# A decode-attention kernel rewritten as a hand-ordered pipeline over blocks of 4 heads, with the softmax shift taken from GpSimd to TensorE

## The chip, the cores and the metric

The kernel runs on one core of a Trainium2 chip. The metric is device time in microseconds (us), as the median of several executions. A run more than 1.5% above the fastest of its kernel counts as slow, and is left out of the times below. Runs were made on several chips of the same kind, and the kernel before was always run again beside the new one: its median was 8688 us at first.

Engines in the profiles: PE is TensorE, PEld its weight load, DVE is VectorE, ACT is ScalarE, POOL is GpSimd, SP issues the DMA transfers. POOLq is GpSimd's sequencer, which takes the instructions in. The granted clock is the share of TensorE's full clock that the throttle let through, as the profile reports it.

## The reference

Two independent attention blocks, A and B, each decode one token for a batch of 8 with 32 heads, over a cache of 4096 keys of 128 elements, all in bf16:

```python
q = (x @ wq)                                    # 8 x 1024 @ 1024 x 4096, then (8, 32, 1, 128)
scores = einsum("bhqd,bhkd->bhqk", q, k_cache) * (128 ** -0.5)
p = softmax(scores)                             # over 4096 keys
o = einsum("bhqk,bhkd->bhqd", p, v_cache)
out = o.reshape(8, 1, 4096) @ wo                # 8 x 1024; A and B are joined on the last axis
```

There are 2 x 8 x 32 = 512 (block, batch, head) units. Each reads its own K and V, 1 MiB each, exactly once. With the weights that is 1107 MB, and nothing can be reused.

## The kernel before

K of a unit lies in SBUF as 128 partitions x 32 keys x 128 elements. The scores are made by a DVE multiply with the broadcast query (L452), a DVE add that folds 128 elements to 64 (L469), four PE matmuls with the identity that sum groups of 16 (L477), and a DVE reduce of the last 16 (L484). Then comes the softmax, for each unit by itself, and PV in eight PE matmuls (L541) into one column tile (the output partitions that `tile_position` names):

```python
o1 = g.add("dve", lambda e: e.tensor_reduce(rmax[:, ur:ur + 1], src, AX.X, ALU.max), ...)           # L505
o2 = g.add("pool", lambda e: e.partition_all_reduce(gmax[:, ur:ur + 1], rmax[:, ur:ur + 1], 128,
                                                    bass.bass_isa.ReduceOp.max), ...)               # L507
o3 = g.add("pool", lambda e: e.tensor_scalar(negb[:, ur:ur + 1], gmax[:, ur:ur + 1],
                                             -scale, None, ALU.mult), ...)                          # L510
o4 = g.add("act", lambda e: e.activation(pT[:, u % PR, :], src, ACTF.Exp, bias=negb[:, ur:ur + 1],
                                         scale=scale, accum_out=rsum[:, ur:ur + 1]), ...)           # L513
...
for gq in range(g0, g1):
    last = e.matmul(pbank[32 * q4:32 * q4 + 4, 0:512], pT[:, u % PR, 4 * gq:4 * gq + 4],            # L541
                    V_sb[:, vslot, gq * 512:(gq + 1) * 512],
                    start=(gq == 0), stop=(gq == NG - 1), tile_position=(0, 32 * q4))
```

o2 and o3 run both on GpSimd, one after the other. The first is a reduction over the 128 partitions. The second multiplies 128 numbers by a constant. Once per head (8 units) GpSimd also adds up the softmax sums with a `partition_all_reduce` (L521).

The order of the instructions on each engine is found by a list scheduler in the kernel's source. It is given a duration for each operation: 0.45 us for the all-reduce, 0.22 us for negb. K has 8 slots in SBUF and V 6, the scores have 3, and each transfer brings two units.

Of the kernel before, what the change touches and what calls it, by code (L numbers as in the profile page):

```python
# [13 lines left out]
class _Op:  # L14
    __slots__ = ("eng", "emit", "deps", "dur", "name", "prio", "dma_key", "nbytes",
                 "token", "sig", "start", "end", "done", "idx", "nsched", "users", "slack", "lock")

    def __init__(self, eng, emit, deps, dur, name, prio, dma_key=None, nbytes=0):
        self.eng = eng
        self.emit = emit  # L20
        self.deps = [d for d in deps if d is not None]
        self.dur = dur
        self.name = name
        self.prio = prio
        self.dma_key = dma_key
        self.nbytes = nbytes
        self.token = None
        self.sig = False
        self.start = None
        self.end = None  # L30
        self.done = None
        self.idx = None
        self.nsched = 0
        self.users = []
        self.slack = 0.0
        self.lock = (eng == "pool")


class _Graph:
    def __init__(self):  # L40
        self.ops = []

    def add(self, eng, emit, deps=(), dur=0.1, name="", prio=0.0, dma_key=None, nbytes=0):
        op = _Op(eng, emit, list(deps), dur, name, prio, dma_key, nbytes)
        self.ops.append(op)
        return op


def _schedule(ops, cfg):
    SEM_LAT = cfg.get("sem_lat", 0.15)  # L50
    DMA_US_PER_MB = cfg.get("dma_us_per_mb", 2.72)
    DMA_LAT = cfg.get("dma_lat", 1.4)
    DMA_MARGIN = cfg.get("dma_margin", 5.0)
    W_EXTRA = cfg.get("w_extra", 25.0)
    for i, op in enumerate(ops):
        op.idx = i
        op.nsched = 0
        op.users = []
    for op in ops:
        for d in op.deps:  # L60
            d.users.append(op)
    eng_free = {e: 0.0 for e in ENGINES}
    dma_free = [0.0]
    lock_free = [0.0]
    avail = {e: [] for e in ENGINES}
    for op in ops:
        if not op.deps:
            avail[op.eng].append(op)
    order = {e: [] for e in ENGINES}
    n_left = len(ops)  # L70
    while n_left:
        best = None
        best_key = None
        for e in ENGINES:
            lst = avail[e]
            if not lst:
                continue
            ef = eng_free[e]
            for op in lst:
                r = 0.0  # L80
                for d in op.deps:
                    t = d.done + SEM_LAT
                    if t > r:
                        r = t
                r += op.slack
                st = r if r > ef else ef
                if op.lock and lock_free[0] > st:
                    st = lock_free[0]
                if e == "sp":
                    kt = dma_free[0] - DMA_MARGIN  # L90
                    key = (st if st > kt else kt, op.prio, op.idx, st)
                else:
                    key = (st, op.prio, op.idx, st)
                if best_key is None or key < best_key:
                    best_key = key
                    best = op
        op = best
        e = op.eng
        st = best_key[3]
        op.start = st  # L100
        op.end = st + op.dur
        eng_free[e] = op.end
        if op.lock:
            lock_free[0] = op.end
        if op.dma_key is not None:
            s0 = max(dma_free[0], op.end + (DMA_LAT if dma_free[0] < op.end else 0.2))
            s1 = s0 + op.nbytes / 1048576.0 * DMA_US_PER_MB
            dma_free[0] = s1
            op.done = s1 + 0.3
            if op.dma_key == "w" and op.slack > 0:  # L110
                op.done += W_EXTRA
        else:
            op.done = op.end
        avail[e].remove(op)
        order[e].append(op)
        n_left -= 1
        for u in op.users:
            u.nsched += 1
            if u.nsched == len(u.deps):
                avail[u.eng].append(u)  # L120
    if cfg.get("verbose"):
        print("SCHED makespan", max(op.done for op in ops), {e: round(sum(o.dur for o in order[e]), 1) for e in ENGINES})
    return order


def _build_kernel(nc, caches, out, cfg):
    NK = cfg.get("NK", 8)
    NV = cfg.get("NV", 6)
    PR = cfg.get("PR", 8)
    SR = cfg.get("SR", 3)  # L130
    AR = cfg.get("AR", 3)
    MW = cfg.get("MW", 64)
    TREE = cfg.get("tree", 1)
    EVS = cfg.get("evac_splits", 2)
    kinds_pat = cfg.get("kinds", "F")
    PAIR = cfg.get("pair", True)
    if PAIR:
        assert NK % 2 == 0 and NV % 2 == 0

    x0, k0, v0, wq0, wo0 = caches[0]  # L140
    B, Sq, D = x0.shape
    _, H, Sk, Dh = k0.shape
    assert Sq == 1 and Dh == 128 and Sk == 4096 and D % 128 == 0
    T = Sk // 128
    G = 4
    DC = D // 128
    HD = H * Dh
    N = B * H
    NC = len(caches)
    NT = NC * N  # L150
    assert NT <= 512 and N % 4 == 0 and (4 % B == 0 or B % 4 == 0)
    scale = float(Dh) ** -0.5
    WH = cfg.get("w_parts", 2)
    assert H % WH == 0
    HP = H // WH
    WSZ = max(DC * HP * Dh, HP * D)
    PW = min(512, D)
    NPH = D // PW
    assert D % PW == 0 and 2 * N <= 512

    kind = [kinds_pat[u % len(kinds_pat)] for u in range(NT)]
    if "P" in kinds_pat:
        for u in range(max(0, NT - cfg.get("tail_p", 2)), NT):
            kind[u] = "P"
        for u in range(min(NT, cfg.get("head_p", 1))):
            kind[u] = "P"
    else:
        for u in range(max(0, NT - cfg.get("tail_e", 4)), NT):
            kind[u] = "E"
        for u in range(min(NT, cfg.get("head_e", 2))):  # L170
            kind[u] = "E"
    p_units = [u for u in range(NT) if kind[u] == "P"]
    d_units = [u for u in range(NT) if kind[u] in "DEF"]
    e_units = [u for u in range(NT) if kind[u] in "EF"]
    e_index = {u: i for i, u in enumerate(e_units)}
    HAS_P = bool(p_units)
    assert not (HAS_P and e_units), "P and E units are mutually exclusive (PSUM budget)"
    p_index = {u: i for i, u in enumerate(p_units)}
    d_index = {u: i for i, u in enumerate(d_units)}

    es = ExitStack()
    with es:
        block = es.enter_context(nc.Block())
        sb = lambda name, shape, dt: es.enter_context(nc.sbuf_tensor(name, shape, dt))
        ps = lambda name, shape, dt: es.enter_context(nc.psum_tensor(name, shape, dt))
# [3 lines left out]
        selA = sb("selA", [128, 128], BF16)  # L189
        selB = sb("selB", [128, 128], BF16)  # L190
        E4 = sb("E4", [128, 4, 4], BF16)
        QB = sb("QB", [128, NC * WH, 4 * HP * B + MW], BF16)
        accS = sb("accS", [128, AR, 512], BF16)
        x_sb = sb("x_sb", [B, NC, D], BF16)
        xT_sb = sb("xT_sb", [128, NC * DC * B], BF16)
        W_sb = sb("W_sb", [128, WSZ], BF16)
        qT_sb = sb("qT_sb", [128, NC, N], BF16)
        K_sb = sb("K_sb", [128, NK, T * Dh], BF16)
        V_sb = sb("V_sb", [128, NV, T * Dh], BF16)
        KT_sb = sb("KT_sb", [128, 2, T * 128], BF16) if HAS_P else None  # L200
        NPB = cfg.get("prod_bufs", 2)
        prod = sb("prod", [128, NPB, T * Dh], BF16)
        qbc = sb("qbc", [128, 2, 4, 128], BF16)
        s_sb = sb("s_sb", [128, SR, T], FP32)
        RS = min(NT, cfg.get("stat_ring", 64))
        assert RS % B == 0 and RS >= 4 * B
        rmax = sb("rmax", [128, RS], FP32)
        gmax = sb("gmax", [128, RS], FP32)
        negb = sb("negb", [128, RS], FP32)
        rsum = sb("rsum", [128, RS], FP32)  # L210
        Lall = sb("Lall", [128, RS], FP32)
        pT = sb("pT", [128, PR, T], BF16)
        rl = sb("rl", [128, 4, B], FP32)
        oacc = sb("oacc", [B, NC, D], FP32)
        on_sb = sb("on_sb", [128, NC, H, B], BF16)
        orow = sb("orow", [B, NC, D], BF16)

        RB = cfg.get("red_banks", 3)
        if HAS_P:
            kt_all = ps("kt_all", [128, 4, 512], FP32)  # L220
            sc = [ps(f"sc{i}", [128, 512], FP32) for i in range(2)]
            ktb_all = kt_all.bitcast(BF16)
            red_ps = None
        else:
            kt_all = ktb_all = None
            red_ps = ps("red_ps", [128, RB, 512], FP32)
            sc = [None, ps("sc1", [128, 512], FP32)]
            if cfg.get("acc_banks", 2) == 2 and RB <= 3:
                sc.append(ps("sc2", [128, 512], FP32))
# [6 lines left out]
        for e in ENGINES[1:]:  # L236
            sems[e] = es.enter_context(nc.semaphore(f"c_{e}"))
# [548 lines left out]
```

## Time and profile before

| | before |
|---|---|
| time, median | 8688 us |
| per unit (divided by 512) | 17.0 us |
| DVE busy | 2145 us, 25% |
| PE busy | 2577 us, 30% |
| packets of the main DMA queue | 32.2% of 16 engines' time, 127 GB/s mean |

No engine is near its limit. These are lines of the page of before: the span, busy time by engine, the main DMA queue, the shares of the chain of waits, and the groups of PV, GpSimd's two groups and exp. A group's line ends with the idle time of its engine just before it, and with what ended most of that idle time.

```profile
span 8728.2 us, 23766 instructions
PE 2576.8 (30%) x7848; PEld 630.1 (7%) x7848; DVE 2145.2 (25%) x2211; ACT 583.7 (7%) x1665; POOL 623.9 (7%) x1104
...
q1 hardware_dynamic: 152448, 1107.40, 32.2%
...
issue 67%; PE 15%; DVE 8%; POOL 7%; ACT 3%; POOLq 1%; DMA 0%; SPq 0%; DVEq 0%; ACTq 0%
...
L541 PE MATMUL sc<-V_sb,pT 128*4 128x512 bf16 x4096 | 1541.1, 580 | 4944.0 <-ACT pT L513 4907.5
...
L507 POOL PARTITION_ALL_REDUCE gmax<-rmax x512 | 455.7, 890 | 3077.8 <-issue 1364.1
...
L513 ACT ACTIVATE pT<-s_sb,negb 128x32 bf16<-128x32 f32 x512 | 164.5, 321 | 6630.9 <-POOL negb L510 6630.9
L510 POOL TENSOR_SCALAR negb<-gmax 128x1 f32<-128x1 f32 x512 | 138.7, 271 | 4624.5 <-issue 4624.5
...
```

"issue" is time for which the profile shows no instruction and no wait. It is 67% of the chain. PE waits for exp and exp waits for negb. Before negb GpSimd is silent for 4624.5 us, 9.0 us per unit, and before the all-reduce for 3077.8 us, 6.0 us per unit.

This is the chain of waits of before over one unit, in order of time: start, length, what.

```profile
4007.48 0.27 POOL negb L510
4007.75 0.02 issue
4007.77 0.42 ACT pT L513 x2
4008.19 0.04 issue
4008.24 1.87 PE sc L541 x4
4010.10 1.83 PE red_ps L477 x4
4011.94 0.02 issue
4011.96 0.70 DVE s_sb L484
4012.66 0.96 issue
4013.63 0.40 POOL gmax L507
4014.02 0.07 POOLq L510 x2
4014.10 6.88 issue
4020.97 0.27 POOL negb L510
```

It looks like a ring: negb, exp, PV, the next unit's score matmuls (their operand was ready at 4000.42, but they stand behind PV on PE), the reduce, the all-reduce, silence, negb. Two lines of the timeline show that the maximum of the scores reduced at 4011.96 is taken only after the all-reduce has begun:

```profile
4013.63 0.40 POOL L507 PARTITION_ALL_REDUCE gmax<-rmax  x1 [5.89 <-DVE s_sb L484]
...
4013.70 0.18 DVE L505 TENSOR_REDUCE rmax<-s_sb 128x1 f32<-128x32 f32 x1
```

That all-reduce works on the maximum before, which had been ready since 4000.58, for 13.0 us. Over the whole trace, with maxima and all-reduces matched in order, 478 of the 512 all-reduces start more than 10 us after their maximum was ready (17.0 us in the median). So the maxima wait for GpSimd, and from 4007.75 to 4013.63 something else must have kept GpSimd, which shows nothing there. What it is, the chain cannot say.

### The profile page before, as it was taken

What the parts mean: (1) busy time and instruction counts of PE and PEld (TensorE: products, weight loads), DVE (VectorE), ACT (ScalarE), POOL (GpSimd) and SP (SyncE); (2) the same over time, 40 slices, a digit from 0 to 9 for tenths busy, and PEclk for the clock granted to TensorE, in tenths of its full rate; (3) what the DMA queues carried; (4) which work ended last, traced back from release to release, by engine and by line L of the source; (5) the groups of instructions that cost most, each with busy time, mean ns of one, the idle gap of its engine ahead of it and who ended that gap; (6) DMA issues with size and microseconds to landing.
All of it is one profiled execution on the core that took longest, in us unless ns stands there. A gap on an engine that the chain in (4) does not pass through costs nothing.

```text
span 8728.2 us, 23766 instructions
## 1 busy us (share of the span) xinstructions
PE 2576.8 (30%) x7848; PEld 630.1 (7%) x7848; DVE 2145.2 (25%) x2211; ACT 583.7 (7%) x1665; POOL 623.9 (7%) x1104
## 2 busy tenths in 40 slices
PE   2232233222232323223332232332323223233233
PEld 0000000000000000000000000000000000000000
DVE  2222222222222222222222222222222222222221
ACT  0000000000000000000000000000000000000000
POOL 0000000000000000000000000000000000000000
PEclk6556656565555655656555555555555555556556
DMA  5332323233332323323233333323333332323231
GB/s 231 135 144 107 134 115 135 115 126 124 135 135 116 135 116 128 122 115 135 116 140 129 118 132 122 129 116 122 128 134 135 127 123 116 135 116 135 116 135 58
DMA packets 152571, 1108.91 MB, mean 127 GB/s; under 512 B 9056, under 2 KB 9056, under 8 KB 21376
## 3 DMA queue, kind: packets, MB, share of 16 engines
q1 hardware_dynamic: 152448, 1107.40, 32.2%
q8 instruction: 62, 1.02, 0.0%
q14 instruction: 61, 0.50, 0.0%
HBM read 1107.33 MB, written 0.03 MB: 127 GB/s over the span
## 4 chain that ended last, share of the span: by engine, by line
issue 67%; PE 15%; DVE 8%; POOL 7%; ACT 3%; POOLq 1%; DMA 0%; SPq 0%; DVEq 0%; ACTq 0%
PE sc L541 7%; PE red_ps L477 7%; POOL gmax L507 5%; DVE s_sb L484 3%; DVE prod L469 3%; DVE prod L452 2%; ACT pT L513 2%; POOL negb L510 2%; PE misc L630 1%; ACT accS L548 1%; POOLq L510 0%; DVE rmax L505 0%; POOL Lall L521 0%; DVE oacc L640 0%; ACT qbc L668 0%
## 5 line engine op out<-in xcount | busy, mean ns | idle before, releaser
L541 PE MATMUL sc<-V_sb,pT 128*4 128x512 bf16 x4096 | 1541.1, 580 | 4944.0 <-ACT pT L513 4907.5
L484 DVE TENSOR_REDUCE s_sb<-red_ps 128x32 f32<-128x512 f32 x512 | 352.4, 688 | 4856.1 <-PE red_ps L477 4856.1
L452 DVE TENSOR_TENSOR prod<-K_sb,qbc 128x4096 bf16<-128x4096 bf16 x512 | 1166.2, 2281 | 28.7 <-ACT qbc L668 28.0
L477 PE MATMUL red_ps<-prod,ident 128*128 128x512 bf16 x2072 | 922.8, 600 | 446.3 <-DVE prod L469 429.5
L541 PEld LDWEIGHTS sc<-V_sb,pT 128*4 128x4 bf16 x4096 | 321.5, 105 | 6075.1 <-ACT pT L513 5205.9
L507 POOL PARTITION_ALL_REDUCE gmax<-rmax x512 | 455.7, 890 | 3077.8 <-issue 1364.1
L469 DVE TENSOR_TENSOR prod<-prod 128x2048 bf16<-128x2048 bf16 x506 | 614.1, 1217 | 1.4
L513 ACT ACTIVATE pT<-s_sb,negb 128x32 bf16<-128x32 f32 x512 | 164.5, 321 | 6630.9 <-POOL negb L510 6630.9
L510 POOL TENSOR_SCALAR negb<-gmax 128x1 f32<-128x1 f32 x512 | 138.7, 271 | 4624.5 <-issue 4624.5
L606 DVE RECIPROCAL rl<-Lall 128x8 f32<-128x8 f32 x64 | 13.0, 203 | 1538.0 <-POOL Lall L521 1538.0
L548 ACT ACTIVATE accS<-sc 4x512 bf16<-4x512 f32 x512 | 300.3, 586 | 1325.4 <-PE sc L541 1322.0
L477 PEld LDWEIGHTS red_ps<-prod,ident 128*128 128x128 bf16 x2072 | 223.2, 128 | 1074.1 <-issue 565.0
L556 PE MATMUL o_ps<-E,accS 128*128 128x4 bf16 x512 | 33.5, 170 | 635.3 <-ACT accS L548 635.3
L513 ACT ACTIVATION_READ_ACCUMULATOR pT<-s_sb,negb 128x1 f32 x512 | 95.3, 186 | 0.0
L505 DVE TENSOR_REDUCE rmax<-s_sb 128x1 f32<-128x32 f32 x512 | 91.6, 179 | 2.1
L668 ACT ACTIVATE qbc<-misc 128x512 bf16<-128x512 f32 x128 | 75.7, 592 | 181.3 <-PE misc L662 175.8
L662 PE MATMUL misc<-ident,qT_sb 128*128 128x128 bf16 x512 | 67.1, 273 | 58.0 <-ACT qbc L668 38.8
L556 PEld LDWEIGHTS o_ps<-E,accS 128*128 128x128 bf16 x512 | 24.1, 103 | 719.2 <-ACT accS L548 713.1
L630 PE MATMUL misc<-W_sb,on_sb 128*8 128x512 bf16 x128 | 55.5, 576 | 49.5 <-DVE on_sb L610 35.7
L521 POOL PARTITION_ALL_REDUCE Lall<-rsum x64 | 27.3, 426 | 387.7 <-issue 308.4
L662 PEld LDWEIGHTS misc<-ident,qT_sb 128*128 128x128 bf16 x512 | 39.1, 118 | 129.5 <-ACT qbc L668 55.5
L640 DVE TENSOR_TENSOR oacc<-oacc,misc 8x512 f32<-8x512 f32 x28 | 18.9, 675 | 48.9 <-PE misc L630 48.9
(25 smaller groups left out, 63.4 us busy)
## 6 DMA issues: line engine op xcount, KB each, us to landing
K_sb<-in_A_k_cache_dram SPq DMA_DIRECT2D x128, 2048.0 KB, 12.3
V_sb<-in_A_v_cache_dram SPq DMA_DIRECT2D x128, 2048.0 KB, 7.6
K_sb<-in_B_k_cache_dram SPq DMA_DIRECT2D x126, 2048.0 KB, 12.3
V_sb<-in_B_v_cache_dram SPq DMA_DIRECT2D x126, 2048.0 KB, 7.5
W_sb<-in_A_wq_dram SPq DMA_DIRECT2D x16, 512.0 KB, 13.9
W_sb<-in_B_wq_dram SPq DMA_DIRECT2D x16, 512.0 KB, 8.6
W_sb<-in_A_wo_dram SPq DMA_DIRECT2D x8, 1024.0 KB, 11.1
W_sb<-in_B_wo_dram SPq DMA_DIRECT2D x8, 1024.0 KB, 10.4
```

Of the source, the lines that this page charges most:

```text
L452: lambda e: e.tensor_tensor(pv_, K_sb[:, kslot, :].rearrange("p (t d) -> p t d", d=Dh), qbc[:, gi % 2, i, :].unsqueeze(1).to_broadcast([12 ...
L469: lambda e: e.tensor_tensor(pv_[:, :, 0:Dh // 2], pv_[:, :, 0:Dh // 2], pv_[:, :, Dh // 2:Dh], ALU.add),
L477: last = e.matmul(red_ps[:, rb, :].rearrange("p (t w) -> p t w", w=EW), ident[:], pj[:, :, jq, :], start=(jq == 0), stop=(jq == nj - 1))
L484: lambda e: e.tensor_reduce(s_sb[:, di % SR, :], red_ps[:, rb, :].rearrange("p (t w) -> p t w", w=EW), AX.X, ALU.add),
L505: o1 = g.add("dve", lambda e: e.tensor_reduce(rmax[:, ur:ur + 1], src, AX.X, ALU.max), [opScore[u], opArmax.get(u - RS)], 0.22, f"rmax{u}" ...
L507: o2 = g.add("pool", lambda e: e.partition_all_reduce(gmax[:, ur:ur + 1], rmax[:, ur:ur + 1], 128, bass.bass_isa.ReduceOp.max), [o1, opNeg ...
L510: o3 = g.add("pool", lambda e: e.tensor_scalar(negb[:, ur:ur + 1], gmax[:, ur:ur + 1], -scale, None, ALU.mult), [o2, opExp.get(u - RS)], 0 ...
L513: o4 = g.add("act", lambda e: e.activation(pT[:, u % PR, :], src, ACTF.Exp, bias=negb[:, ur:ur + 1], scale=scale, accum_out=rsum[:, ur:ur ...
L541: last = e.matmul(pbank[32 * q4:32 * q4 + 4, 0:512], pT[:, u % PR, 4 * gq:4 * gq + 4], V_sb[:, vslot, gq * 512:(gq + 1) * 512], start=(gq ...
L548: opAcc[u] = g.add("act", lambda e: e.activation(accS[32 * q4:32 * q4 + 4, ring, :], pbank[32 * q4:32 * q4 + 4, 0:512], ACTF.Copy), [opPV[ ...
L630: last = e.matmul(misc[0:B, 0:PW], on_sb[:, c, hh, :], W_sb[:, hl * D + ph * PW: hl * D + (ph + 1) * PW], start=(hh == h0), stop=(hh == h1 ...
L662: last = e.matmul(misc[:, i * 128:(i + 1) * 128], qT_sb[:, cc, jj:jj + 1].to_broadcast([128, 128]), ident[:], start=True, stop=True)
```

## The change

Its intent is to make one fixed order by hand in place of the scheduler's, with PV 6 units behind the multiply; to make the shift for 4 units at once, and on TensorE (a transpose of the 128x4 row maxima, a DVE max, and a tiny matmul that broadcasts and multiplies by -scale) in place of GpSimd; and to put the eight PV matmuls of a unit in four column tiles, to run side by side. The softmax sums also go to a PE matmul with ones. wq is loaded for 4 heads at a time (1 KB packets). The diff replaces nearly the whole builder, so only its core is shown:

```diff
-    NK = cfg.get("NK", 8)
-    NV = cfg.get("NV", 6)
-    PR = cfg.get("PR", 8)
-    SR = cfg.get("SR", 3)
+    LAG = 6
+    NK, NV, NP = 8, 8, 3
+    PR = 8
+    SG = 3
...  (softmax shift)
-            o2 = g.add("pool", lambda e: e.partition_all_reduce(gmax[:, ur:ur + 1], rmax[:, ur:ur + 1], 128, bass.bass_isa.ReduceOp.max),
-            o3 = g.add("pool", lambda e: e.tensor_scalar(negb[:, ur:ur + 1], gmax[:, ur:ur + 1], -scale, None, ALU.mult),
+        def make_tr(g):
+            opTr[g] = add("pe", lambda e: e.transpose(misc[0:HB, 0:128], rmax[:, g % 2, :], ident32[:]),
+                          [opRmax[g], c_ident32, last["misc"]])
+        def make_gm(g):
+            opGm[g] = add("dve", lambda e: e.tensor_reduce(gm[:, g % 2:g % 2 + 1], misc[0:HB, 0:128], AX.X, ALU.max),
+                          [opTr[g], _at(opNegb, g - 2)])
+        def make_exp(g):
+            opNegb[g] = add("pe", lambda e: e.matmul(misc[:, 128:128 + HB], gm[:, g % 2:g % 2 + 1].to_broadcast([HB, 128]),
+                                                     nid[:], start=True, stop=True), [opGm[g], c_nid])
+            opNegS[g] = last["misc"] = add("act", lambda e: e.activation(negb[:, g % 2, :], misc[:, 128:128 + HB], ACTF.Copy),
+                                           [opNegb[g], _at(opExp, HB * (g - 2) + HB - 1)])
...  (PV)
-                        last = e.matmul(pbank[32 * q4:32 * q4 + 4, 0:512], pT[:, u % PR, 4 * gq:4 * gq + 4], V_sb[:, vslot, gq * 512:(gq + 1) * 512],
-                                        start=(gq == 0), stop=(gq == NG - 1), tile_position=(0, 32 * q4))
+                for r in range(2):
+                    for q in range(4):
+                        gq = 2 * q + r
+                        i = e.matmul(bank[32 * q:32 * q + 4, :], pT[:, u % PR, 4 * gq:4 * gq + 4],
+                                     V_sb[:, u % NV, gq * 512:(gq + 1) * 512],
+                                     start=(r == 0), stop=(r == 1), tile_position=(0, 32 * q))
...  (order)
-        order = _schedule(g.ops, cfg)
+        for s in range(NT + LAG + 4):
+            if s < NT:
+                make_mul(s)
...  (K loads)
+            if 0 <= s - LAG < NT:
+                u = s - LAG
+                make_pv(u)
...  (V loads)
+            if 1 <= s <= NT:
+                make_red(s - 1)
+            if r4 == 1 and 1 <= g4 <= NG:
+                make_gm(g4 - 1)
+                make_exp(g4 - 1)
...
+            if s < NT:
+                make_eacc(s, make_fold(s))
+            if r4 == 0 and 1 <= g4 <= NG:
+                make_rmax(g4 - 1)
+                make_tr(g4 - 1)
...
```

## The prediction

> **What bounds the kernel now.** No engine does: the page's first part gives PE 30%, DVE 25%, ACT 7%, POOL 7%, and DMA packets 32% of 16 engines' time. 8688 us over 512 (batch, head) units is 17.0 us per unit. It is a latency ring through GpSimd. The chain of waits from 4000 to 4060 us repeats one loop per unit: exp 0.42 us, four PV matmuls 1.87, four score matmuls (L477) 1.83, score reduce (L484) 0.69, often the fold 1.14, PARTITION_ALL_REDUCE issued 0.4, then 6.9 or 11.1 us of "issue", then negb 0.27. The waits view sums the silence before negb to 4624.5 us, 9.0 per unit; "issue" is 67% of the chain. I read it as all-reduce time not recorded. PE runs in order and has the next unit's score matmuls behind this unit's PV, which waits for exp, so the latency is paid on every unit.
>
> **What the change does.** The 512 GpSimd all-reduces and 512 negb become, for each 4 units, a PE transpose, a DVE max, a tiny matmul and an ACT copy. PV of a unit runs 6 units behind its multiply, so this latency lies beside two or more steps of DVE work.
>
> **Work per unit afterwards (durations of the trace).**
> - DVE: multiply 2.28 + fold 1.22 + reduce 0.69 + about 0.14 (larger rmax and new gm, estimates from the 0.18 us rmax) = 4.33 us, some 4.5 with gaps: 2220 us busy, 2300 if it bounded.
> - PE: eight PV matmuls took 3.7 us cold; four column tiles side by side should need about 1 us (estimate; the Trainium skill, "TensorE: Matmul & The Clock Gate", Part 3, measures 2.38x for three; no run here shows it yet). With score matmuls at most 1.9 us and small work, 2.5 to 3.3 us.
> - ACT: exp 0.51, accS 0.59, qbc and negb 0.2: 1.3 us.
> - DMA: bytes are the same, 1107 MB. From 20 to 60 us the trace shows a saturated stretch: DMA share 1.01, 417 to 420 GB/s. So 2.10 MB per unit take 5.02 us.
>
> DMA becomes the bound. The skill's "HBM Reference", Access, gives about 425 GB/s for a core streaming alone; the trace agrees. 1107 MB at 418 is 2650 us. The wq loads fall to 1 KB packets; 2, 4 and 8 KB packets take 84, 159 and 309 ns (medians), so 1 KB should take about 46: wq and wo together add some 11 us. Start 5 us, tail 10 us. Sum 2676; for imperfect saturation I say 2700 us, 3.2 times faster.
>
> Range 2640 to 2880: the upper end is 385 GB/s sustained.
>
> **Signs.** DMA share at 0.97 or more and 405 to 420 GB/s in nearly all of the 40 slices; POOL under 10 us; the chain mostly DMA and PE/DVE links with K_sb or V_sb DMA as releasers, no POOL; DVE busy about 2220 us (82%), its largest wait the K_sb DMA before the multiply; PV matmuls of one unit spanning about 1 us; K landing times rising from 12 us to 25 or more.
>
> **What would make it wrong.** Sustained HBM rate below the 40-us stretch; the ring of 4 K and 4 V pairs on one in-order issue queue not keeping requests outstanding; column tiles not overlapping, with PE at the low clock (5.6 us per unit, then PE-bound near 2900); DVE stretched past 5 us by semaphore waits between dependent instructions; the transpose chain outlasting the pipeline's slack.

## The result, and the profile after

The kernel after takes 2664.0 us (median of 4 runs, 2663.85 to 2664.39), the kernel before beside it 8696.8 us. The ratio is 0.3063 (95% interval 0.3054 to 0.3072). The prediction was 2700 us, with a range of 2640 to 2880.

Lines of the page of after: span, busy time, the DMA engines' busy tenths and GB/s in 40 slices, the main queue, the chain's shares, and groups on DVE and PE.

```profile
span 2662.3 us, 22669 instructions
PE 1603.4 (60%) x9008; PEld 444.1 (17%) x9008; DVE 2103.0 (79%) x1829; ACT 575.2 (22%) x1811; POOL 4.1 (0%) x18
...
DMA  9999999999999999999999999999999999999998
GB/s 393 414 421 421 421 415 417 421 422 421 414 419 421 421 421 411 419 421 422 421 410 419 421 421 421 412 419 421 421 421 411 419 421 421 421 421 418 421 421 340
...
q1 hardware_dynamic: 164320, 1107.40, 100.6%
...
DMA 89%; PE 5%; DVE 4%; SPq 1%; issue 1%; ACT 0%; DVEq 0%
...
L237 DVE TENSOR_TENSOR prod<-K_sb,qbc 128x4096 bf16<-128x4096 bf16 x512 | 1170.0, 2285 | 110.7 <-DMA K_sb<-in_A_k_cache_dram 59.7
L297 PE MATMUL pv<-V_sb,pT 128*4 128x512 bf16 x4096 | 516.2, 581 | 846.4 <-DMA V_sb<-in_B_v_cache_dram 424.9
...
```

The DMA engines are full from the first slice to the last. 1107 MB at 421 GB/s is 2630 us; the rest is the start, a slower last 10 us and the tail after the last V. Silence is gone from the chain ("issue" 1%), and what PE waits for before PV is now the V transfer. The Trainium skill, "HBM Reference", Specifications, gives about 425 GB/s for a core that streams alone; the trace has 421 in the undisturbed slices.

Two lines of the timeline of after, for PV and for the score matmuls of one step (start, length, engine, what, how many):

```profile
1300.48 1.02 PE L297 MATMUL pv<-V_sb,pT 128*4 128x512 bf16 x8 [3.95 <-DMA V_sb<-in_A_v_cache_dram]
...
1302.17 1.89 PE L252 MATMUL red<-prod,ident 128*128 128x512 bf16 x4
...
```

Eight matmuls in column tiles take 1.02 us where four full ones of the same length take 1.89. In one tile eight take 3.7 (twice the 1.87 of before, also at a low granted clock). So the four tiles do overlap, 3.6 times, and the prediction's 1 us was right.

So far everything agrees with the prediction. But the change does at least four things at once, and the total does not say which of them earned the 6000 us. The prediction named a cause, and that can be tested by doing one part alone on the kernel before, or undoing one part of the kernel after.

### The profile page after: what moved, and what is told of

Read it like the earlier page. It is cut to its first block, busy times and chain, and to the rows that moved or that the text cites. A ratio compares the mean times of both kernels' runs of the same rounds, so it can differ in the third digit from the quotient of the medians.

```text
span 2662.3 us, 22669 instructions
## 1 busy us (share of the span) xinstructions
PE 1603.4 (60%) x9008; PEld 444.1 (17%) x9008; DVE 2103.0 (79%) x1829; ACT 575.2 (22%) x1811; POOL 4.1 (0%) x18
## 3 DMA queue, kind: packets, MB, share of 16 engines
q1 hardware_dynamic: 164320, 1107.40, 100.6%
## 4 chain that ended last, share of the span: by engine, by line
DMA 89%; PE 5%; DVE 4%; SPq 1%; issue 1%; ACT 0%; DVEq 0%
DMA V_sb<-in_A_v_cache_dram 46%; DMA V_sb<-in_B_v_cache_dram 42%; PE red L252 3%; DVE prod L244 2%; DVE prod L237 2%; PE pv L297 1%; DMA K_sb<-in_A_k_cache_dram 1%; SPq L151 1%; DVE s_sb L258 1%; PE misc L227 0%; PE o L309 0%; PE proj L331 0%; DMA WQ<-in_A_wq_dram 0%; PE misc L215 0%; DVE gm L272 0%
## 5 line engine op out<-in xcount | busy, mean ns | idle before, releaser
L297 PE MATMUL pv<-V_sb,pT 128*4 128x512 bf16 x4096 | 516.2, 581 | 846.4 <-DMA V_sb<-in_B_v_cache_dram 424.9
L252 PE MATMUL red<-prod,ident 128*128 128x512 bf16 x2048 | 830.2, 551 | 185.9 <-DVE prod L244 185.9
L302 ACT ACTIVATE accS<-pv 128x512 bf16<-128x512 f32 x512 | 305.6, 597 | 1949.5 <-PE pv L297 1895.4
L258 DVE TENSOR_REDUCE s_sb<-red 128x32 f32<-128x512 f32 x512 | 351.5, 687 | 425.9 <-PE red L252 424.6
L252 PEld LDWEIGHTS red<-prod,ident 128*128 128x128 bf16 x2048 | 202.1, 120 | 496.8 <-issue 246.3
L297 PEld LDWEIGHTS pv<-V_sb,pT 128*4 128x4 bf16 x4096 | 62.9, 81 | 1192.7 <-issue 787.0
L309 PEld LDWEIGHTS o<-E,accS 128*128 128x128 bf16 x2048 | 91.4, 104 | 319.1 <-issue 314.6
L309 PE MATMUL o<-E,accS 128*128 128x1 bf16 x2048 | 133.9, 169 | 0.5 <-ACT accS L302 0.5
L227 PE MATMUL misc<-q_sb,selb 8*128 8x512 bf16 x128 | 76.2, 595 | 0.8 <-ACT q_sb L221 0.8
L276 PE MATMUL misc<-nid,gm 4*128 4x4 f32 x256 | 58.6, 297 | 14.9 <-DVE gm L272 13.6
```

The lines of the kernel that those rows point to most:

```text
L227: opQb[g] = add("pe", lambda e: e.matmul(misc[:], selb[:, b, :], q_sb[:, blk % 4, :], start=True, stop=True), [c_selb, opQs[blk], last["mi ...
L252: i = e.matmul(dst, ident[:], v[:, :, j, :], start=(j == 0), stop=(j == 3))
L258: opRed[u] = add("dve", lambda e: e.tensor_reduce(s_sb[:, g % SG, i, :], red_ps[u % 2][:, :].rearrange("p (t w) -> p t w", w=16), AX.X, AL ...
L276: opNegb[g] = add("pe", lambda e: e.matmul(misc[:, 128:128 + HB], gm[:, g % 2:g % 2 + 1].to_broadcast([HB, 128]), nid[:], start=True, stop ...
L297: i = e.matmul(bank[32 * q:32 * q + 4, :], pT[:, u % PR, 4 * gq:4 * gq + 4], V_sb[:, u % NV, gq * 512:(gq + 1) * 512], start=(r == 0), sto ...
L302: opAcc[u] = add("act", lambda e: e.activation(accS[:, u % 2, :], bank[:], ACTF.Copy), [opPV[u], _at(opExt, u - 2)])
```

## The experiments

The theory of the prediction, called A, is that the all-reduce has a long latency which the ring makes every unit pay. The first rival, B, is that the scheduled order, the small rings and PV in one tile cost most. Twelve kernels were run. The kernels made from before go through its scheduler again, which may put the remaining operations in another order.

### The shift taken out of the kernel before

A softmax does not change with its shift, and these scores are far below 1, so a shift of zero is correct here.

```diff
-            o1 = ... rmax        (DVE)
-            o2 = ... all-reduce  (GpSimd)
-            o3 = ... negb        (GpSimd)
-            o4 = ... ACTF.Exp, bias=negb[:, ur:ur + 1], ...   [o3, ...]
+            o4 = ... ACTF.Exp, bias=zb[:], ...                [opScore[u], op_zb, ...]     # zb: zeros, set once
```

> Kernel before without rmax, all-reduce and negb; the exp takes a constant zero as its bias (the softmax does not change with the shift, and these scores are far below 1). Theory A (the silent GpSimd time is a ring that every unit pays): the 7 to 14 us per unit vanish, the kernel ends at 2700 to 3300 us, bound by DMA at about 5.0 us per unit or by PE in one column tile (3.7 + 1.9 us cold). Rival B (the list-scheduled order of PE and the small rings cost most, whatever the shift does): still above 5000 us.

Measured: 2663.8 us, correct, ratio 0.3077 (0.3069 to 0.3086). That is the time of the kernel after, with the old order, the old rings and PV in one column tile. Rival B is out: none of the rest of the change is worth anything while DMA bounds. Its page shows the same full DMA queue:

```profile
span 2662.2 us, 20221 instructions
...
q1 hardware_dynamic: 152448, 1107.40, 100.4%
...
```

The end of the expectation failed on the good side: PE in one tile does not bound either. Its 3.7 + 1.9 us were read at a low granted clock; the mean here was 0.79, against 0.59 in the kernel before.

### The shift kept, but nobody waits for it

```diff
-            o4 = ... ACTF.Exp, bias=negb[:, ur:ur + 1], ...   [o3, ...]
+            o4 = ... ACTF.Exp, bias=zb[:], ...                [o1, op_zb, ...]
```

> Kernel before with rmax, all-reduce and negb kept for every unit, but exp reads a constant zero, so nothing waits for GpSimd. Theory A1 (GpSimd's own rate, one all-reduce per unit, 7.3 us without DMA traffic and 11 to 14 with it): bound by GpSimd, because rmax and the scores wait for ring places behind it, at 8 to 13 us per unit, 4100 to 6700 us. Rival A2 (only the latency in the ring costs, GpSimd could take several at once or quicker): as b_noshift, below 3300 us.

Measured: 8130.7 us, correct, ratio 0.9388 (0.9356 to 0.9420). The ring is cut, and only 6% is gained. Theory A falls: the latency in a ring is not what set the time. GpSimd needs 15.9 us per unit (8130.7 / 512) even when nothing depends on the result; the other engines run ahead and then stop, until GpSimd has caught up with the sums of each head (DVE waits 5633.1 us for them) and with the places in its rings. The time was above the range expected, so "an all-reduce at 7 to 14 us" was too simple. The chain of waits of this run shows why:

```profile
4020.45 0.26 POOL negb L512
4020.71 0.31 issue
4021.02 0.01 POOLq L509
4021.03 0.02 issue
4021.05 0.01 POOLq L509
4021.07 10.93 issue
4032.00 0.38 POOL gmax L509
4032.37 0.07 POOLq L512 x2
4032.44 6.65 issue
4039.09 0.26 POOL negb L512
```

There are two silences per unit, not one: one of 6.65 us between the all-reduce and negb, and one of 10.93 us between negb and the next all-reduce. Each begins after a pair of POOLq entries. In the trace these are records named MODIFY_POOL_CONFIG, which the page doesn't count as busy. The kernel before has 2052 of them, in pairs: two pairs for each unit, one on the way from an all-reduce to the multiply, and one on the way back. The kernel after has 2.

That gives theory C: GpSimd exchanges its program whenever it goes from `partition_all_reduce` to an ordinary instruction or back, and each exchange takes 6 to 12 us. The Trainium skill, "GPSIMD Engine Reference", section 2.1, says that "the first call to a freshly-loaded kernel additionally pays an IRAM-load of approximately 6 µs", with no visible profile instruction. It says this of a first call; here it would be paid at each of some 1026 exchanges. What is exchanged the profile does not show; "exchange" is used below for the pair of records and the silence after it.

### The scheduler's numbers and the score slots changed

```diff
-            o2 = ... 0.45, f"armax{u}", prio)
+            o2 = ... 10.0, f"armax{u}", prio)
-            o3 = ... 0.22, f"negb{u}", prio)
+            o3 = ... 0.27, f"negb{u}", prio)
+            o2.lock = o3.lock = False
-    SR = cfg.get("SR", 3)
+    SR = cfg.get("SR", 6)
```

> Kernel before with only its scheduler's numbers changed: all-reduce 10 us in place of 0.45, GpSimd not locked against VectorE, six score slots in place of three; every operation is kept. Rival B (order is the cause): PE no longer has the next score matmuls behind the waiting PV, and the time falls to what GpSimd's own rate allows, the time of b_poolside, 4100 to 6700 us. Theory A as a pure ring: over 8000 us. If it lands at b_poolside, order explains the part from 8690 down to there and GpSimd's rate the rest.

Measured: 4782.8 us, correct, ratio 0.5526 (0.5505 to 0.5547). It is far below the 8130.7 us of the run before it, so it did not land "at the time of b_poolside", and GpSimd's rate is not a fixed time per unit. The timeline of GpSimd in this run explains it:

```profile
2010.35 2.32 POOL L507 PARTITION_ALL_REDUCE gmax<-rmax  x2 [7.10 <-DVE s_sb L484]
2019.38 0.55 POOL L510 TENSOR_SCALAR negb<-gmax 128x1 f32<-128x1 f32 x2 [6.71 <-issue]
2026.94 1.13 POOL L507 PARTITION_ALL_REDUCE gmax<-rmax  x2 [7.01 <-issue]
2035.48 0.55 POOL L510 TENSOR_SCALAR negb<-gmax 128x1 f32<-128x1 f32 x2 [7.41 <-issue]
```

With these changes the scheduler happens to put two all-reduces and then two multiplies; which of the changes (duration, lock, score slots) made it do so was not told apart. The second of each follows at once (two multiplies in 0.55 us). The silences are as long as before, but there are half as many: 1028 MODIFY_POOL_CONFIG records in place of 2052, and 55% of the time. The same operations are all there. What counts is how often GpSimd changes from one kind to the other.

### The multiply moved off GpSimd, all else as before

```diff
-            o3 = g.add("pool", lambda e: e.tensor_scalar(negb[:, ur:ur + 1], gmax[:, ur:ur + 1], -scale, None, ALU.mult),
+            o3 = g.add("act", lambda e: e.activation(negb[:, ur:ur + 1], gmax[:, ur:ur + 1], ACTF.Copy, scale=-scale),
```

> Kernel before with one operation moved: negb (a 128x1 multiply by a constant) goes from GpSimd to ScalarE; the 512 all-reduces stay on GpSimd, the ring and its order stay. New theory C (GpSimd swaps its program whenever it goes from an all-reduce to an ordinary instruction and back, 6 to 12 us each way; the trace of before has 2052 MODIFY_POOL_CONFIG records, two per swap, that is two swaps per unit): all but a few such records vanish and the kernel runs at 2664 to 2800 us. Theory A (the latency of the all-reduce itself, 7 to 14 us, in a ring): above 6000 us.

Measured: 2671.7 us, correct, ratio 0.3086 (0.3079 to 0.3093). One line, one operation on another engine, and the kernel before is within 0.3% of the kernel after. All 512 all-reduces are still on GpSimd, still in the ring, still one per unit. The trace has 4 MODIFY_POOL_CONFIG records. This is GpSimd's group line in that run:

```profile
L507 POOL PARTITION_ALL_REDUCE gmax<-rmax x512 | 736.1, 1438 | 1799.5 <-DVE rmax L505 1799.5
```

An all-reduce takes 1.44 us in the mean, and GpSimd's idle time is now a wait for work. This settles theory C against A: the all-reduce itself is not what was slow.

### GpSimd put back into the kernel after

Three kernels give the shift of the kernel after back to GpSimd, one all-reduce for 4 units. The first also has the multiply on GpSimd:

```diff
-            opTr[g] = add("pe", lambda e: e.transpose(...))          # and gm on DVE, negb on PE, copy on ACT
+            opTr[g] = add("pool", lambda e: e.partition_all_reduce(gmx[:, g % 2, :], rmax[:, g % 2, :], 128,
+                                                                   bass.bass_isa.ReduceOp.max), ...)
+            opNegS[g] = add("pool", lambda e: e.tensor_scalar(negb[:, g % 2, :], gmx[:, g % 2, :], -scale, None, ALU.mult), ...)
```

> Kernel after with the shift of 4 units made by one GpSimd all-reduce and one GpSimd multiply in place of the PE transpose, DVE max, PE matmul and ACT copy; order and lag of 6 units unchanged. Theory (GpSimd needs 11 to 14 us under full DMA, the lag leaves about 6 us): PV of the first unit of each group comes some 6 us late, VectorE has 3 us of slack per group, so 2900 to 3400 us. Rival (batching 4 units is enough, TensorE is not needed): 2664 us within 1%.

Measured: 2990.0 us, correct, ratio 0.3454 (0.3441 to 0.3466), as expected. Divided by 128 groups it is 23.4 us per group. GpSimd's two groups are:

```profile
L269 POOL PARTITION_ALL_REDUCE gmx<-rmax x128 | 286.4, 2237 | 1352.9 <-DVE rmax L265 1330.0
...
L272 POOL TENSOR_SCALAR negb<-gmx 128x4 f32<-128x4 f32 x128 | 33.1, 259 | 1303.0 <-issue 1303.0
```

They add up to (286.4 + 1352.9 + 33.1 + 1303.0) / 128 = 23.2 us, but this proves nothing, since busy and idle time of one engine always add up to the span. What decides is when the all-reduce starts. The two MODIFY_POOL_CONFIG records come 0.3 us after the multiply, and yet in 118 of the 128 groups the all-reduce starts 0.14 us after DVE's rmax has ended. So this exchange was over in time, and the profile's 1330.0 us of waiting for rmax are a true wait (unlike in the kernel before, where the maxima had long been ready). The period is a loop: the exchange before the multiply (1303.0 / 128 = 10.2 us), then exp, PV and the next scores up to rmax (1352.9 / 128 = 10.6 us), then the all-reduce. It is a latency that the lag does not cover, as the expectation said, but the exchange makes it, not the all-reduce. DMA is busy for 94% of the span; whether that is why an exchange takes 10 us here is tested below.

The second kernel leaves more time for the latency:

```diff
-    LAG = 6
+    LAG = 10
-    PR = 8
+    PR = 16
```

> a_pool4 with the lag from multiply to PV raised from 6 to 10 units and the ring of weights pT from 8 to 16. Theory C (a_pool4 is bound by GpSimd's rate, two swaps per group of 4, 23.4 us per group): no change, 2900 to 3000 us. Theory A (a_pool4 is bound by the latency that a lag of 6 cannot cover): 2664 us within 1%, since 4 more units are 20 us.

Measured: 2809.8 us (median of three runs; the fourth took 2839.1 us), correct, ratio 0.3242 (0.3227 to 0.3257). Both expectations missed: theory A said 2664, theory C said no change from 2990. GpSimd still has 514 records. But now in 124 of the 128 groups the all-reduce starts later than 0.3 us after its rmax, 2.7 us in the median: the maxima wait for GpSimd. So the longer lag did take away the loop, which was worth 180 us, and behind it stands GpSimd's rate, with two exchanges per group: (133.7 + 1230.8 + 40.7 + 1390.8) / 128 = 21.8 of 22.0 us. The recorded all-reduce also got shorter (1.04 us in place of 2.24); why was not tested.

The third kernel is a_pool4 (lag 6) with the multiply on ScalarE:

```diff
-            opNegS[g] = add("pool", lambda e: e.tensor_scalar(negb[:, g % 2, :], gmx[:, g % 2, :], -scale, None, ALU.mult), ...)
+            opNegS[g] = add("act", lambda e: e.activation(negb[:, g % 2, :], gmx[:, g % 2, :], ACTF.Copy, scale=-scale), ...)
```

> a_pool4 (lag 6) with the multiply for negb on ScalarE in place of GpSimd, so GpSimd runs all-reduces only, one per 4 units, under full DMA. Theory C (swaps of GpSimd's program cost, the all-reduce itself is under 3 us): no swaps, 2664 us within 0.5%. Rival (an all-reduce on GpSimd is slow in itself, so TensorE was needed): above 2750 us, as a_pool4 and a_pool4_lag10 were.

Measured: 2664.3 us, correct, ratio 0.3085 (0.3077 to 0.3092), and 4 records. GpSimd does as well as the TensorE transpose, as long as it does nothing else between two all-reduces.

### DMA taken away from the kernel before

In the timeline of before, 87 silences before negb were looked at (from 4000 to 5500 us) with what DMA moved in each. In 46 of them DMA moved less than 50 GB/s, and their mean is 7.02 us (6.69 to 7.83). In 41 it moved more than 250 GB/s, and their mean is 11.29 us (7.49 to 13.47). Two of the windows, each from an all-reduce to its negb (window and its length, busy time of the engines, granted clock, DMA share, GB/s):

```profile
4013.63:4020.97 7.34, 0.48 (x5) 0.23 (x4) 2.45 (x3) 1.06 (x2) 0.39 (x1) 0.73 0.01 2
4027.28:4038.81 11.53, 0.00 (x0) 0.00 (x0) 2.32 (x3) 0.56 (x1) 0.38 (x2) 0.65 0.88 351
```

To see whether that is a cause, the kernel before was run with K and V loaded for the first slots only and used again; the result is wrong.

```diff
-                    opK[u] = opK[u + 1] = dma(
+                    opK[u] = opK[u + 1] = opK[kslot] if u >= NK else dma(
-                    opV[u] = opV[u + 1] = dma(
+                    opV[u] = opV[u + 1] = opV[vslot] if u >= NV else dma(
```

> Kernel before with only the first 8 K and 6 V units loaded and used again (wrong result on purpose): DMA is idle nearly all the time, every instruction and both GpSimd swaps per unit stay. If DMA traffic stretches a swap (in before 7.5 us where DMA moved nothing, 10 to 13 where it moved over 300 GB/s): every swap to negb takes about 7 us, the time falls to 13.5 us per unit, 6700 to 7100 us. If a swap's length has nothing to do with DMA: 8600 to 8700 us.

Measured: 7636.0 us, ratio 0.8840 (0.8810 to 0.8869). The group of negb:

```profile
L510 POOL TENSOR_SCALAR negb<-gmax 128x1 f32<-128x1 f32 x512 | 140.5, 274 | 3597.6 <-issue 3597.6
```

The silence is 3597.6 / 512 = 7.03 us, the 7.02 of the quiet half of before. It was 9.03, and 2.0 us x 512 is 1024 us; the time fell by 991 us (8627.4 to 7636.0). The records are again 2052. So DMA traffic does stretch an exchange. The silence before the all-reduce hardly changed (3077.8 to 3042.8 us), because in the kernel before little DMA falls into it; in b_poolside it is 6.04 us in the mean where DMA moved less than 50 GB/s, and 9.62 us where it moved more than 250. The Trainium skill, "GPSIMD Engine Reference", section 1.1, says that a loadable program of GpSimd is brought in by DMA, which would fit; the profile does not show that transfer, so why it is stretched stays open. The total expected, 6700 to 7100 us, was missed, because it was worked out from the shortest round of the ring (13.5 us) and a mean round is 14.9.

### What the other parts of the change are worth

First the column tiles, undone in the kernel after:

```diff
-                for r in range(2):
-                    for q in range(4):
-                        gq = 2 * q + r
-                        i = e.matmul(bank[32 * q:32 * q + 4, :], ..., start=(r == 0), stop=(r == 1), tile_position=(0, 32 * q))
+                for gq in range(8):
+                    i = e.matmul(bank[0:4, :], ..., start=(gq == 0), stop=(gq == 7), tile_position=(0, 0))
```

> Kernel after with the eight PV matmuls of a unit in one column tile, one behind the other. If DMA bounds (theory): 2664 us within 0.5%, PE busier and at a higher granted clock than 0.62. If the column tiles were needed to keep PE under DMA: 2800 us or more.

Measured: 2667.3 us, correct, ratio 0.3080 (0.3071 to 0.3089): 3.3 us, or 0.1%, more than the kernel after. PE is busy for 74% of the span at a granted clock of 0.85, in place of 60% at 0.62. Why the clock is higher was not tested.

Then DMA is relieved of V: only the first 8 V units are loaded.

```diff
-                if u % 2 == 1 and u - 1 + NV < NT:
+                if False:
                     load_v(u - 1 + NV)
-            opPV[u] = add("pe", emit, [opExp[u], opV[u], ...
+            opPV[u] = add("pe", emit, [opExp[u], opV[u % NV], ...
```

> Kernel after with only the first 8 V units loaded and used again for all others (wrong result on purpose), so DMA moves 587 MB in place of 1107 MB. If DMA bounds the kernel after, time falls to VectorE's own rate, 4.3 to 4.6 us per unit, 2200 to 2400 us. If something behind DMA (a wait between engines) bounds: above 2500 us.

Measured: 2122.8 us, ratio 0.2451 (0.2445 to 0.2457), and below the range expected. Its output is wrong, which doesn't matter for the time.

```profile
PE 1357.6 (64%) x9008; PEld 419.9 (20%) x9008; DVE 2075.8 (98%) x1829; ACT 576.1 (27%) x1811; POOL 4.1 (0%) x18
```

DVE is busy for 98%, at 4.15 us per unit. So DMA is what bounds the kernel after, DVE stands next, 540 us below it, and the hand-made order leaves DVE hardly any hole. The same cut in the old kernel without a shift:

> b_noshift (the old order, small rings, PV in one column tile, no shift at all) with only the first 6 V units loaded (wrong result on purpose), so DMA no longer bounds; to be held beside a_fewv, 2123 us. If the hand order and the column tiles are worth something once DMA is out of the way: 2250 to 2700 us, with VectorE waiting for PE. If they are not: within 3% of 2123 us, since VectorE has no max work here.

(The edit is that of b_noshift, with V loaded as in b_nodma and K as before.) Measured: 2297.3 us, ratio 0.2660 (0.2654 to 0.2666), wrong. DVE is busy for 90%; its largest wait is for the score matmuls, as expected, but that is only 53 us. So the scheduler's order with its one-tile PV and smaller rings is 174 us or 8% slower than the hand-made kernel (2297.3 / 2122.8), once DMA is out of the way, and although it makes no maxima. The four parts of that difference (order, rings, tiles, and where the sums are made) were not told apart.

### Larger wq packets

```diff
-        WQ = sb("WQ", [128, 2, DC, HB * Dh], BF16)
+        WQ = sb("WQ", [128, DC, HM * Dh], BF16)
-            for f in halves:
-                opWQ[(m, f)] = dma(WQ[:, f], ... 4 heads ...)
+            opWQ[(m, 0)] = opWQ[(m, 1)] = dma(WQ[:], ... 8 heads ...)
```

> Kernel after with the two 1 MB wq loads of 8 heads joined in one of 2 MB, so that 16416 packets of 1 KB become half as many of 2 KB. From the trace of after (48 ns for 1 KB, 88 ns for 2 KB, 16 engines): 16416 x 48 / 16 = 49 us become 45 us. If DMA bounds and packet time adds up: 4 to 6 us faster, 2658 to 2660 us. If it does not: 2664 us as after.

Measured: 2660.0 us (2659.76 to 2660.35), correct, ratio 0.3080 (0.3072 to 0.3087). The kernel after had 2663.85 to 2664.39 in another set of runs, and a_pool4_act, whose DMA is that of the kernel after, had 2663.9 to 2664.7 in this set. So 4 us were gained, as packet time predicts: in the trace 16384 packets of 1 KB became 8192 of 2 KB (32 of the 16416 are not wq), and 16384 x 48 ns / 16 = 49 us, against 8192 x 88 / 16 = 45 us. It is the fastest correct kernel of this study, by 0.15%: far under the 2% that the record asks for to call a kernel faster, though the runs do not overlap.

### The exchanges in one table

| kernel | MODIFY_POOL_CONFIG records | time, us |
|---|---|---|
| before | 2052 | 8697 |
| before, nobody waits for the shift | 2050 | 8131 |
| before, no DMA | 2052 | 7636 |
| before, other scheduler numbers and six score slots | 1028 | 4783 |
| after, all-reduce and multiply of 4 units on GpSimd | 514 | 2990 |
| the same, lag 10 | 514 | 2810 |
| before, multiply on ScalarE | 4 | 2672 |
| before, no shift | 4 | 2664 |
| after, all-reduce on GpSimd, multiply on ScalarE | 4 | 2664 |
| after | 2 | 2664 |

Half the number of records, divided into the time, gives 7.4 to 11.6 us per exchange in the first six rows. The other rows are at DMA's bound. The four runs that are not in the table have 2 or 4 records.

## Why the prediction was right or wrong

- **The time was right**, 2664.0 us against 2700. It was right because it was worked out from what bounds the kernel afterwards, and for that nothing needs to be known of why the kernel before was slow. DMA took 421 GB/s in place of the 418 read from a stretch of 40 us, and the queue stayed full, so the allowance for imperfect saturation wasn't needed.
- **DMA as the next bound** was right: 100.6% of 16 engines' time in the main queue, and without the V loads the time falls to 2123 us.
- **The cause named for before was wrong.** The step that failed is "It is a latency ring through GpSimd", with "I read it as all-reduce time not recorded" and "so the latency is paid on every unit". With exp no longer waiting for GpSimd the kernel still takes 8131 us, and in the trace of before the maxima wait for GpSimd (17.0 us in the median). The silence is not the all-reduce (1.44 us in the mean, when GpSimd does all-reduces only) but two exchanges per unit, 9.0 and 6.0 us. The prediction counted one silence and gave the time of the other to PV, the score matmuls and the reduce. These did run in that time, but GpSimd's 6.0 us of exchange ran beside them.
- **"This latency lies beside two or more steps of DVE work"**, as the reason why the change helps, was wrong as well. With the lag and the batches of 4 and the work still on GpSimd, the lag does not cover the latency and the kernel takes 2990 us, and a longer lag brings 2810 and not 2664. It is the absence of exchanges that helps. Here the prediction was lucky: its account would have promised much the same time for that kernel, and nothing in it says that the multiply had to leave GpSimd.
- **The column tiles** were costed rightly (1.02 us for the predicted 1 us), and the prediction was right not to count on them: one tile costs 3.3 us in all. The fear of "PE at the low clock (5.6 us per unit)" did not come true with one tile: the granted clock was 0.85.
- **DVE** was expected at 2220 us busy (82%), and shows 2103 (79%); its groups alone sum to 2211, so the term was right and the page counts overlapping instructions once. The bound of 2300 us was too high: 2123 us was measured without the V loads.
- **The wq and wo term**, 11 us, was of the right size: 48 ns for 1 KB against 46 expected, and joining packets gained 4 us.
- **Signs**: DMA share, POOL at 4 us, a chain of DMA, and K landing after 33 us (12 before) all came. DVE's largest wait was to be the K transfer; it was the score matmuls (425 us), with K at 102, and it is PE that waits for V (845 us).

## What to carry to other kernels

Look on GpSimd for silent time between instructions of different kinds, add it up over all of that engine's groups, and count the records of its configuration. Where the profile names a release for that time, look when the released operand was ready: long before in the kernel before, 0.14 us before in a_pool4. If GpSimd alternates between a partition all-reduce and ordinary instructions, move the ordinary ones to another engine before anything else is rewritten: here one moved multiply gave 3.2 times, and a whole rewrite gave 0.3% more. A chain of waits shows a path that could set the time, not that it does; check that each link is a dependency, cut the path in an experiment, and see whether the time follows.

## What the Trainium skill lacked or had wrong

- The Trainium skill, "GPSIMD Engine Reference", section 2.1, gives about 6 us for the first call to a freshly loaded kernel. It lacks that alternating between a partition all-reduce and an ordinary instruction brings a silence of this size each time, and in both directions: 7.03 us before the multiply, and 5.9 to 6.2 us before the all-reduce in the timeline, in the run without DMA; 15.0 us per unit in b_poolside.
- The same page lacks that DMA traffic stretches it: 7.02 us with DMA quiet and 11.29 us with DMA above 250 GB/s in the same run, and 10.2 us before the multiply in a_pool4.
- The same page, section 4.1, recommends GpSimd for a reduction over partitions. That held here (2664.3 us with it, 2664.0 with the TensorE transpose), but it doesn't warn of mixing it with other work on the same engine (2990.0 us).
- "TensorE: Matmul & The Clock Gate", Part 3, has 2.38 times for three column tiles and no figure for four column tiles. Four column tiles of 128x512 gave about 3.6 times here, at a low granted clock (1.02 us for eight matmuls against 3.7).
- "DMA: Bandwidth & Descriptors", Specifications, gives 512 B and more as the minimum transfer for line rate. Here a 1 KB packet took 48 ns and an 8 KB packet 312 ns (medians), which is 21.3 and 26.3 GB/s per engine: 1 KB runs at 81% of the rate of 8 KB.
